# A streamed decode step on one core: the first keys in two loads, the score product ahead of the value product, and the last loads of the stream rearranged

## The chip, the core and the metric

The kernel runs on one core of a Trainium2 chip. The metric is the device time of one execution in microseconds (us). The kernel before takes 384.94 us, the median of 3 runs (384.27 to 385.3).

The core has a matrix engine (PE in the profile, with its weight loads as PEld), a vector engine (DVE), a scalar engine (ACT), a general engine (POOL) and a synchronisation engine (SP) that here only starts DMA transfers. Each engine works through its own list of instructions in order; they meet at semaphores. Data come from the chip's main memory by 16 DMA engines into the on-chip memory (SBUF); products of PE land in a small accumulator memory (PSUM).

## The reference

Two tokens (B = 2 batch rows of one position each, D = 448) are layer-normalised. The first branch is a grouped attention over a cache: 16 query heads, 8 key/value heads, 4096 cached positions, head size 256. The second is a bilinear gate. The output is `x + s * silu(h @ w_down)`:

```python
def _A_ref(x, k_cache, v_cache, wq, wo):
    ...
    scores = jnp.einsum("bhqd,bhkd->bhqk", q, k) * (Dh ** -0.5)
    p = _softmax(scores, axis=-1)
    o = jnp.einsum("bhqk,bhkd->bhqd", p, v)
    return ... @ wo
def _B_ref(x, w_gate, w_up, w_down):
    g = jnp.einsum("bsd,df->bsf", x, w_gate)
    u = jnp.einsum("bsd,df->bsf", x, w_up)
    return jnp.einsum("bsf,fd->bsd", g * u, w_down)
xn = _layernorm(x)
s = _A_ref(xn, A_k_cache, A_v_cache, A_wq, A_wo)
g = _silu(_B_ref(xn, B_w_gate, B_w_up, B_w_down))
return x + s * g
```

Everything is float32. The caches hold 2 x 8 x 4096 x 256 keys and as many values, 134 MB together; the weights are 24 MB more. Each number read takes part in one or two multiplications only.

## The kernel before, in words

**Steps.** The attention is cut into N = 16 steps, one for each pair of a key/value head and a batch row. Step i needs the keys k_i (128 x 8192 floats, 4 MB) and the values v_i (4 MB). For each step the program does:

- `scores(i)` on PE (line 344): 16 products of 128x512 from the scaled query copies `qs` (made by POOL, line 153) and k_i, into the PSUM tile `s`.
- the largest score: DVE's `maximum(i)` reduces `s` to `m` (line 242); PE turns that column to a row (`sm`, line 348); DVE reduces the row (`mx`, line 244); PE spreads it back (line 350); DVE scales and negates it (line 248).
- ACT's `exps(i)` (line 173) writes the exponentials `p` and their sums `su`; DVE adds the sums into `sr` (line 252).
- `turn(i)` on PE (line 300) transposes `p` into the two PSUM tiles `pt`, and sums the denominators (line 356). DVE copies one half to `pT` (line 255), ACT the other (line 178); DVE takes the reciprocal (line 257).
- `values(i, v)` on PE (line 366): 16 products of 128x512 from `pT` and v_i, into the PSUM tile `o`. ACT copies `o` to `ob` (line 185); `join(i)` on PE (line 374) folds it into `oc`; DVE's `heads(i)` writes the finished heads to `oT` (line 263).

**Buffers and loads.** There are two large buffers, `buf[0]` and `buf[1]`, of 8 MB each, and `low` (6.3 MB). SP issues all large loads, in one order (lines 120 to 135): the gate and up weights to `low`, `w_down` to `buf[1]`, `wq` to `buf[0]`; then the first 8 MB of the cache, which hold k_0 and k_1, to `buf[1]`; then 14 loads of 8 MB, number i holding v_i and k_(i+2), to `buf[i % 2]`; then v_14 into the first half of `buf[0]` and v_15 into the first half of `buf[1]`; then `w_o` in six pieces of 14, 9, 4, 3, 1 and 1 of its 32 steps. The first three pieces (27 steps) go to `low`, the last three to the second half of `buf[0]` (`late`).

Below, load i is the one that holds v_i and k_(i+2). SP waits ahead of a load until the buffer is free: load 0 for the query product that read `wq`, load i from 1 on for `scores(i)`, the last reader of its buffer. v_14 waits for `scores(14)`, v_15 for `scores(15)`. The `w_o` loads have no wait of their own, but stand behind these on SP.

**PE's order.** PE runs `scores(0)`, `turn(0)`, `scores(1)`, and then a hardware loop of seven passes over two steps each, whose body is for each of the two:

```python
values(i, buf[i][:, :ROW])
turn(i + 1)
join(i)
scores(i + 2, buf[i][:, ROW:])
```

`scores` includes the two small products for the largest score and their waits. After the loop come `values(14)`, `turn(15)`, `join(14)`, `values(15)` and `join(15)`.

**The end.** `w_o` is multiplied by the finished heads. Steps 0 to 26 are summed in `o` on four column groups of PE (line 305). ACT copies that sum to `ys` (line 191), and `spread` (line 309) adds it into `acc`; then the last five steps are multiplied straight into `acc` (line 419), DVE multiplies by the gate and adds x (lines 278 and 281), and SP stores the result (line 135). The order on PE is fixed by the code: 27 steps, `spread`, five steps.

## Time and profile before

| what | value |
|---|---|
| median of 3 runs | 384.94 us (384.27 to 385.3) |
| the profiled execution's own time | 384.97 us |
| its span in the profile | 383.7 us |
| read from main memory | 158.54 MB, 413 GB/s over the span |
| busy share of PE, DVE, ACT, POOL | 58%, 16%, 13%, 1% |
| mean clock granted to PE | 0.795 of full speed |

The span is the stretch from the first to the last recorded instruction; the device time of the same execution is 1.27 us longer. All times in rows of the profile count from the span's start. The waits name the engine (or DMA) whose event came last. In groups of PE's rows, each float32 product is recorded as two matmuls, so 16 products are x32. "PEq" and "issue" as releasers mean that the profile shows no event for the wait, which is where PE waits for a load's semaphore. A table of windows gives for each stretch the busy time of each engine, the clock granted to PE, the mean busy share of the 16 DMA engines and their GB/s; in it a packet counts in the window in which it starts, so windows shorter than a packet can show more than 1.00 or nothing.

### The profile page before, as it was taken

The page shows a single profiled execution, that of the slowest core. Times are in us where ns is not written, and L with a number is a line of the kernel's source. Part 1 is how long each engine was busy: PE and PEld are TensorE (multiplying, and loading weights), DVE is VectorE, ACT ScalarE, POOL GpSimd, SP SyncE. Part 2 cuts the span into 40 slices and gives each one's busy share as a digit, 9 for nine tenths or more (in the row PEclk, how much of TensorE's full clock was granted, in tenths as well). Part 3 has the DMA queues.
Part 4 walks back from the last instruction along what each step waited for, and adds up shares of the span by engine and source line. Part 5 has one row for each costly group of instructions (what it writes and reads, how often), then busy time and mean ns, then how long its engine had stood idle before and what let it go on. Part 6 is the DMA issues. An engine that isn't in the chain of part 4 may idle for free. (4 is left out here: it accounts for less than half of the span.)

```text
span 383.7 us, 3749 instructions
## 1 busy us (share of the span) xinstructions
PE 224.3 (58%) x1642; PEld 88.4 (23%) x1642; DVE 60.3 (16%) x142; ACT 48.8 (13%) x105; POOL 5.0 (1%) x23
## 2 busy tenths in 40 slices
PE   0094363579092929392939383838483847477666
PEld 0021010323040404040403141313131313132322
DVE  3001000321112121212121212120212120212100
ACT  1002020111111111111111111111111111111100
POOL 1000000000000000000000000000000000000000
PEclk9999595889686777887776877786877786878898
DMA  8999999989999999999999999999999999985993
GB/s 336 424 443 456 435 437 437 437 323 432 437 437 432 437 431 437 437 430 418 437 430 410 430 424 430 437 437 437 437 430 437 437 437 437 417 366 222 433 416 142
DMA packets 3915, 158.70 MB, mean 414 GB/s; under 512 B 578, under 2 KB 836, under 8 KB 1092
## 3 DMA queue, kind: packets, MB, share of 16 engines
q1 hardware_dynamic: 3888, 158.59, 96.4%
q8 instruction: 5, 0.08, 0.1%
q10 hardware_dynamic: 20, 0.01, 0.0%
q14 instruction: 2, 0.02, 0.0%
HBM read 158.54 MB, written 0.06 MB: 413 GB/s over the span
## 5 line engine op out<-in xcount | busy, mean ns | idle before, releaser
L366 PE MATMUL o<-buf,pT 128*32 128x512 f32 x512 | 87.0, 841 | 73.5 <-PEq L50 73.5
L344 PE MATMUL s<-buf,qs 128*32 128x512 f32 x512 | 60.7, 616 | 9.4 <-PEq L50 9.4
L366 PEld LDWEIGHTS o<-buf,pT 128*32 128x32 f32 x512 | 22.4, 149 | 125.0 <-issue 124.9
L173 ACT ACTIVATE p<-s,m 128x512 f32<-128x512 f32 x32 | 21.7, 682 | 124.9 <-DVE m L248 124.9
L255 DVE COPY pT<-pt 128x512 f32<-128x512 f32 x16 | 11.1, 692 | 133.1 <-PE pt L300 133.1
L242 DVE TENSOR_REDUCE m<-s 128x1 f32<-128x1024 f32 x16 | 19.6, 1225 | 65.8 <-PE s L344 65.8
L185 ACT COPY ob<-o 128x512 f32<-128x512 f32 x16 | 9.4, 586 | 136.8 <-PE o L366 136.8
L344 PEld LDWEIGHTS s<-buf,qs 128*32 128x32 f32 x512 | 15.5, 113 | 40.5 <-issue 40.3
L300 PE MATMUL pt<-ident,p 128*128 128x128 f32 x128 | 18.3, 289 | 2.1 <-PEq L50 2.1
L300 PEld LDWEIGHTS pt<-ident,p 128*128 128x128 f32 x128 | 14.4, 146 | 14.8 <-issue 14.8
L348 PE MATMUL sm<-ident,m 128*1 128x128 f32 x16 | 4.3, 269 | 23.0 <-PEq L50 23.0
L374 PE MATMUL oc<-sel,ob 128*128 128x2 f32 x128 | 16.5, 251 | 0.8 <-PEq L50 0.8
L374 PEld LDWEIGHTS oc<-sel,ob 128*128 128x128 f32 x128 | 15.6, 192 | 1.7 <-issue 1.7
L350 PE MATMUL sm<-one,mx 1*128 1x1 f32 x32 | 6.6, 273 | 13.8 <-PEq L50 13.8
L291 PE MATMUL s<-low,xnT 128*32 128x448 f32 x48 | 7.0, 730 | 12.5 <-DMA low<-wgu 12.5
L291 PE MATMUL s<-buf,xnT 128*32 128x512 f32 x48 | 6.9, 721 | 9.8 <-DMA buf<-wq 9.8
L244 DVE TENSOR_REDUCE mx<-sm 1x128 f32<-1x512 f32 x16 | 10.9, 678 | 7.2 <-PE sm L348 7.2
L178 ACT COPY pT<-pt 128x512 f32<-128x512 f32 x16 | 9.4, 585 | 8.6 <-PE pt L300 8.6
L348 PEld LDWEIGHTS sm<-ident,m 128*1 128x1 f32 x16 | 1.3, 79 | 37.1 <-issue 37.1
L305 PE MATMUL o<-low,oT 128*32 128x448 f32 x54 | 8.1, 684 | 2.9 <-DMA low<-wo 2.9
L350 PEld LDWEIGHTS sm<-one,mx 1*128 1x128 f32 x32 | 5.7, 222 | 16.8 <-issue 16.8
L252 DVE TENSOR_TENSOR sr<-su 128x128 f32<-128x128 f32 x16 | 4.7, 292 | 24.2 <-ACT p L173 24.2
(65 smaller groups left out, 65.8 us busy)
## 6 DMA issues: line engine op xcount, KB each, us to landing
buf<-vv SPq DMA_DIRECT2D x2, 4096.0 KB, 14.8
buf<-wq SPq DMA_DIRECT2D x1, 7168.0 KB, 42.5
low<-wgu SPq DMA_DIRECT2D x1, 6272.0 KB, 18.1
buf<-wd SPq DMA_DIRECT2D x1, 3136.0 KB, 25.1
low<-wo SPq DMA_DIRECT2D x1, 3136.0 KB, 19.7
low<-wo SPq DMA_DIRECT2D x1, 2016.0 KB, 25.1
low<-wo SPq DMA_DIRECT2D x1, 896.0 KB, 26.8
buf<-wo SPq DMA_DIRECT2D x1, 672.0 KB, 27.7
```

The lines of the kernel that those rows point to most:

```text
L173: ins = e.activation(p[:, h], s[:, h], AF.Exp, bias=m[:, 1:2], scale=1.0 / 16, accum_out=su[:, h:h + 1])
L178: e.copy(pT[:, 1], pt[1]).then_inc(sems["pt"], 1)
L185: e.copy(ob, o).then_inc(sems["ob"], 1)
L242: e.tensor_reduce(m[:, 0:1], s.rearrange("p h n -> p (h n)"), axis=AX.X, op=OP.max).then_inc(sems["m"], 1)
L244: e.tensor_reduce(mx, sm[:1, None, :128].rearrange("p o (c j) -> p o j c", c=NT).to_broadcast([1, NT, W, NT]), axis=AX.X, op=OP.max).then_ ...
L255: e.tensor_copy(pT[:, 0], pt[0]).then_inc(sems["pt"], 1)
L291: e.matmul(t[W * c:W * (c + 1), :n], xnT[:, k, :], block(NT * k + c), start=k == 0, stop=False)
L300: ins = e.transpose(t[:, i, :], a[:, i * 128:(i + 1) * 128], ident)
L344: ins = e.matmul(s[W * c:W * (c + 1), h], qs[i % 2][:, d].rearrange("p j q -> p (j q)"), k[:, h, d, c, :], start=d == 0, stop=d == 1)
L350: pe.ev(e.matmul(sm[:, 128:129], mx.rearrange("p c j -> p (c j)"), one, start=True, stop=True), "x", i)
L366: ins = e.matmul(o[W * at:W * (at + 1), :], pT[:, h, j, 64 * c + 16:64 * c + 48], v[:, h, j, c, :], start=h == 0 and j < 2, stop=h == 1 an ...
L374: ins = e.matmul(oc[:, 2 * d:2 * d + 2], ob[:, h * 256 + d * 128:h * 256 + (d + 1) * 128], sel[:, h], start=h == 0, stop=h == 1)
```

## The change

Five edits go together.

1. **The first 8 MB are two loads of 4 MB**, k_0 and k_1, each with a semaphore of its own. `scores(0)` waits for the first alone, `scores(1)` for the second.
2. **In a step of the loop, `turn(i + 1)` and `scores(i + 2)` stand ahead of `values(i)`**. The two small products for the largest score are parted from `scores` (`highest`, `spread_highest`) and stand inside the value product, after its sixth and its twelfth product. DVE and ACT follow: DVE has its reciprocal and `maximum(i + 2)` ahead of the copy to `pT`, and the sums last; ACT has `exps(i + 2)` ahead of the copy to `ob`. The copies to `pT` now come after `values(i)`, which reads `pT`.
3. **The buffers are given free by `values`**: load i waits from i = 2 on for `values(i - 2)`, since `scores(i)` has read the other half of that buffer earlier.
4. **v_14 and v_15 both go to `buf[0]`**, each with its own semaphore, once `values(12)` is done. The first three `w_o` loads follow without a wait. The last three go to the second half of `buf[1]` in place of `buf[0]` and wait for `values(13)`.
5. **At the end the three `w_o` steps of the fourth piece stand ahead of `spread`**, and only the last two steps behind it.

**PE, one step of the loop** (`o<-buf,pT` is the value product, `s<-buf,qs` the score product, `pt<-ident,p` the transposes, `oc<-sel,ob` the join; t0 is the semaphore of the load). Before:

```order
L366 MATMUL o<-buf,pT 32x512 [waits t0,pt]
L366 MATMUL o<-buf,pT 32x512 x15
L300 MATMUL pt<-ident,p 128x128 [waits sr]
L300 MATMUL pt<-ident,p 128x128 x7
L356 MATMUL sm<-sel,sr 128x2
L374 MATMUL oc<-sel,ob 128x2 [waits ob]
L374 MATMUL oc<-sel,ob 128x2 x3
L344 MATMUL s<-buf,qs 32x512 [waits q]
L344 MATMUL s<-buf,qs 32x512 x15
L348 MATMUL sm<-ident,m 1x128 [waits m]
L350 MATMUL sm<-one,mx 128x1 [waits mx]
```

With the change, the same step:

```order
L315 MATMUL pt<-ident,p 128x128 [waits pt,sr]
L315 MATMUL pt<-ident,p 128x128 x7
L375 MATMUL sm<-sel,sr 128x2
L359 MATMUL s<-buf,qs 32x512 [waits t0,q]
L359 MATMUL s<-buf,qs 32x512 x15
L384 MATMUL o<-buf,pT 32x512 x6
L365 MATMUL sm<-ident,m 1x128 [waits m]
L384 MATMUL o<-buf,pT 32x512 x6
L369 MATMUL sm<-one,mx 128x1 [waits mx]
L384 MATMUL o<-buf,pT 32x512 x4
L392 MATMUL oc<-sel,ob 128x2 [waits ob]
L392 MATMUL oc<-sel,ob 128x2 x3
```

The wait for the load has moved from the value product to the score product, the transposes of the next step stand ahead of it, and the two waits for DVE's maximum now lie within the value product.

**SP, from the cache loads to the store** (`pe` is PE's own count of finished work). Before:

```order
L124 DMA buf<-kv 128x16384 [waits pe]
L127 DMA buf<-kv 128x16384 [waits pe] x14
L130 DMA buf<-vv 128x8192 [waits pe] x2
L133 DMA low<-wo 128x6272
L133 DMA low<-wo 128x4032
L133 DMA low<-wo 128x1792
L133 DMA buf<-wo 128x1344
L133 DMA buf<-wo 128x448 x2
L135 DMA res<-r 128x112 [waits dv]
```

With the change:

```order
L125 DMA buf<-kv 128x8192 [waits pe]
L125 DMA buf<-kv 128x8192
L128 DMA buf<-kv 128x16384 [waits pe] x14
L131 DMA buf<-vv 128x8192 [waits pe]
L131 DMA buf<-vv 128x8192
L136 DMA low<-wo 128x6272
L136 DMA low<-wo 128x4032
L136 DMA low<-wo 128x1792
L136 DMA buf<-wo 128x1344 [waits pe]
L136 DMA buf<-wo 128x448 x2
L138 DMA res<-r 128x112 [waits dv]
```

The second of the last two value loads has lost its wait, and the wait ahead of the `w_o` loads now stands ahead of the fourth of them only.

**PE, the end** (`o<-low,oT` are the first 27 steps of `w_o`, `acc<-ys,pick` is `spread`, `acc<-buf,oT` the last five steps, four products each). As a piece of the difference:

```order
-L305 MATMUL o<-low,oT 32x448 x27
-L309 MATMUL acc<-ys,pick 32x112 x4
-L419 MATMUL acc<-buf,oT 32x112 x20
+L320 MATMUL o<-low,oT 32x448 x27
+L444 MATMUL acc<-buf,oT 32x112 x12
+L324 MATMUL acc<-ys,pick 32x112 x4
+L444 MATMUL acc<-buf,oT 32x112 x8
```

Twelve of the twenty products have moved ahead of `spread`.

The diff:

```diff
--- before.py
+++ after.py
@@ -59,7 +59,7 @@
 
     first = nc.alloc_semaphore("first")
     sems = {n: nc.alloc_semaphore(n) for n in (
-        "x", "xg", "gu", "wd", "wq", "t0", "t1", "pt", "sr", "ob", "q", "m", "mx", "res")}
+        "x", "xg", "gu", "wd", "wq", "k0", "k1", "v14", "v15", "t0", "t1", "pt", "sr", "ob", "q", "m", "mx", "res")}
     won = [nc.alloc_semaphore(f"wo{i}") for i in range(len(ABREAST + DIRECT))]
     pe = Queue(nc, nc.tensor, "pe", known)
     dv = Queue(nc, nc.vector, "dv", known)
@@ -103,7 +103,7 @@
     oc = ps("oc", [128, 512])
     acc = ps("acc", [128, 512])
 
-    late = buf[0][:, ROW:]
+    late = buf[1][:, ROW:]
     bounds = [0]
     for n in ABREAST + DIRECT:
         bounds.append(bounds[-1] + n)
@@ -121,14 +121,17 @@
         e.dma_start(buf[1][:, :14 * D], wd).then_inc(sems["wd"], 16)
         e.dma_start(buf[0][:, :28 * 512], wq).then_inc(sems["wq"], 16)
         sp.after(pe, "y4")
-        e.dma_start(buf[1], kv[0]).then_inc(turns[1], 16)
+        for h in range(2):
+            e.dma_start(buf[1][:, h * ROW:(h + 1) * ROW], kv[0][:, h * ROW:(h + 1) * ROW]).then_inc(sems[f"k{h}"], 16)
         for i in range(N - 2):
-            sp.after(pe, *(("q", 1) if i == 0 else ("s", i)))
+            sp.after(pe, *(("q", 1) if i == 0 else ("s", 1) if i == 1 else ("v", i - 2)))
             e.dma_start(buf[i % 2], kv[1 + i]).then_inc(turns[i % 2], 16)
-        for i in range(N - 2, N):
-            sp.after(pe, "s", i)
-            e.dma_start(buf[i % 2][:, :ROW], vv[i % 2]).then_inc(turns[i % 2], 16)
+        sp.after(pe, "v", N - 4)
+        for h in range(2):
+            e.dma_start(buf[0][:, h * ROW:(h + 1) * ROW], vv[h]).then_inc(sems[f"v{N - 2 + h}"], 16)
         for n, lo, hi in zip(won, bounds, bounds[1:]):
+            if lo == early:
+                sp.after(pe, "v", N - 3)
             t = low[:, lo * D:hi * D] if hi <= early else late[:, (lo - early) * D:(hi - early) * D]
             e.dma_start(t, wo[:, lo * D:hi * D]).then_inc(n, 16)
         sp.after(dv, "res")
@@ -181,12 +184,12 @@
         half(0)
         exps(1)
         for i in range(N):
+            if i + 2 < N:
+                exps(i + 2)
             ac.after(pe, "v", i)
             e.copy(ob, o).then_inc(sems["ob"], 1)
             if i + 1 < N:
                 half(i + 1)
-            if i + 2 < N:
-                exps(i + 2)
         ac.after(pe, "w4")
         ac.ev(e.copy(ys, o[:, :D]), "accs")
 
@@ -247,14 +250,18 @@
             dv.after(pe, "x", i)
             dv.ev(e.tensor_scalar(m[:, 1:2], sm[:, 128:129], -1.0 / 16, None, op0=OP.mult), "neg", i)
 
-        def half(i):
+        def sums(i):
             dv.after(ac, "exp", i)
             e.tensor_tensor(sr, su[:, 0:1].to_broadcast([128, 128]), su[:, 1:2].to_broadcast([128, 128]),
                             op=OP.add).then_inc(sems["sr"], 1)
+
+        def inverse(i):
+            dv.after(pe, "u", i)
+            dv.ev(e.reciprocal(r[i % 2], sm[:, 130:132]), "r", i)
+
+        def half(i):
             dv.after(pe, "t", i, 0)
             e.tensor_copy(pT[:, 0], pt[0]).then_inc(sems["pt"], 1)
-            dv.after(pe, "u", i)
-            dv.ev(e.reciprocal(r[i % 2], sm[:, 130:132]), "r", i)
 
         def heads(i):
             g, b = where(i)
@@ -266,14 +273,22 @@
                 r[i % 2][:, :, None, None].to_broadcast([128, REP, 2, DUP]), op=OP.mult), "oT", i)
 
         maximum(0)
+        sums(0)
         half(0)
+        inverse(0)
         maximum(1)
+        sums(1)
         for i in range(N):
             if i + 1 < N:
+                inverse(i + 1)
+            if i + 2 < N:
+                maximum(i + 2)
+            if i + 1 < N:
+                dv.after(pe, "v", i)
                 half(i + 1)
             heads(i)
             if i + 2 < N:
-                maximum(i + 2)
+                sums(i + 2)
         dv.after(pe, "fin")
         dv.ev(e.tensor_mul(r0, acc[:, :SL], gate), "r0")
         dv.after(dv, "r0")
@@ -304,10 +319,10 @@
             c = i % NT
             return e.matmul(t[W * c:W * (c + 1), :D], lhs, rhs, start=i < NT, stop=i >= total - NT)
 
-        def spread(stop):
+        def spread(start, stop):
             for c in range(NT):
                 ins = e.matmul(acc[W * c:W * (c + 1), :SL], pick.rearrange("p b j -> p (b j)"),
-                               ys[:, c * SL:(c + 1) * SL], start=True, stop=stop)
+                               ys[:, c * SL:(c + 1) * SL], start=start, stop=stop)
             return ins
 
         pe.after(dv, "xn")
@@ -327,7 +342,7 @@
             ins = abreast(o, hT[:, i], buf[1][:, i * D:(i + 1) * D], i, 14)
         pe.ev(ins, "y4")
         pe.after(ac, "ys")
-        pe.ev(spread(True), "y")
+        pe.ev(spread(True, True), "y")
         e.wait_ge(sems["wq"], 16)
         for h in range(2):
             pe.ev(rows(s[:, h], buf[0][:, h * 14 * 512:(h + 1) * 14 * 512], 512), "q", h)
@@ -344,8 +359,12 @@
                         ins = e.matmul(s[W * c:W * (c + 1), h], qs[i % 2][:, d].rearrange("p j q -> p (j q)"),
                                        k[:, h, d, c, :], start=d == 0, stop=d == 1)
             pe.ev(ins, "s", i)
+
+        def highest(i):
             pe.take(sems["m"])
             pe.ev(e.transpose(sm[:1, :128], m[:, 0:1], ident), "m", i)
+
+        def spread_highest(i):
             pe.take(sems["mx"])
             pe.ev(e.matmul(sm[:, 128:129], mx.rearrange("p c j -> p (c j)"), one, start=True, stop=True), "x", i)
 
@@ -355,12 +374,11 @@
                 pe.ev(turned(pt[h], p[:, h]), "t", i, h)
             pe.ev(e.matmul(sm[:, 130:132], sr, sel[:, 0], start=True, stop=True), "u", i)
 
-        def values(i, v):
-            pe.take(turns[i % 2], 16)
-            pe.take(sems["pt"], 2)
+        def values(i, v, between):
             v = v.rearrange("p (h i c n) -> p h i c n", h=2, i=BLK, c=2)
             for h in range(2):
                 for j in range(BLK):
+                    between.get((h, j), lambda: None)()
                     for c in range(2):
                         at = 2 * (j % 2) + c
                         ins = e.matmul(o[W * at:W * (at + 1), :], pT[:, h, j, 64 * c + 16:64 * c + 48],
@@ -375,18 +393,23 @@
                                    start=h == 0, stop=h == 1)
             pe.ev(ins, "j", i)
 
-        pe.take(turns[1], 16)
-        scores(0, buf[1][:, :ROW])
-        turn(0)
-        scores(1, buf[1][:, ROW:])
+        for i in range(2):
+            e.wait_ge(sems[f"k{i}"], 16)
+            scores(i, buf[1][:, i * ROW:(i + 1) * ROW])
+            highest(i)
+            spread_highest(i)
+            if i == 0:
+                turn(0)
 
         at, count = dict(pe.at), pe.n
         with nc.Fori(0, LOOPS, 1, engines=[PE], head_slot={PE: 0}):
             for i in range(2):
-                values(i, buf[i][:, :ROW])
+                pe.take(sems["pt"], 2)
                 turn(i + 1)
+                pe.take(turns[i], 16)
+                scores(i + 2, buf[i][:, ROW:])
+                values(i, buf[i][:, :ROW], {(0, 3): lambda: highest(i + 2), (1, 2): lambda: spread_highest(i + 2)})
                 join(i)
-                scores(i + 2, buf[i][:, ROW:])
         per = pe.n - count
         for key, n in list(pe.at.items()):
             if at.get(key) != n:
@@ -394,13 +417,15 @@
                     pe.at[(key[0], key[1] + 2 * k, *key[2:])] = n + per * k
         pe.n = count + per * LOOPS
 
-        i = N - 2
-        values(i, buf[0][:, :ROW])
-        turn(i + 1)
-        join(i)
-        values(i + 1, buf[1][:, :ROW])
-        pe.after(dv, "oT", i)
-        join(i + 1)
+        for i in range(N - 2, N):
+            pe.take(sems["pt"], 2)
+            if i == N - 2:
+                turn(N - 1)
+            else:
+                pe.after(dv, "oT", N - 2)
+            e.wait_ge(sems[f"v{i}"], 16)
+            values(i, buf[0][:, (i - N + 2) * ROW:(i - N + 3) * ROW], {})
+            join(i)
         pe.after(dv, "gate")
 
         def left(i):
@@ -417,11 +442,12 @@
                 else:
                     for c in range(NT):
                         ins = e.matmul(acc[W * c:W * (c + 1), :SL], left(i), wo_step(i)[:, c * SL:(c + 1) * SL],
-                                       start=False, stop=i == WO - 1)
+                                       start=lo == early and i == lo, stop=i == WO - 1)
             if hi == early:
                 pe.ev(ins, "w4")
+            if lo == early:
                 pe.after(ac, "accs")
-                spread(False)
+                spread(False, False)
         pe.ev(ins, "fin")
 
     pool_side()
```

## The prediction

> **What bounds the kernel now.** I read the DMA part of the page first, because the kernel reads 158.54 MB and PE is busy for little more than half of the span.
>
> ```profile
> DMA  8999999989999999999999999999999999985993
> GB/s 336 424 443 456 435 437 437 437 323 432 437 437 432 437 431 437 437 430 418 437 430 410 430 424 430 437 437 437 437 430 437 437 437 437 417 366 222 433 416 142
> q1 hardware_dynamic: 3888, 158.59, 96.4%
> ```
>
> Each slice is 383.7 / 40 = 9.59 us. Most stand near 437 GB/s; four stand out: the ninth (323), those from 335.7 us on (366, 222) and the last (142). The bytes are the same after the change, so time can only come from such holes, or go into new ones. Next I read PE in order of time, at the places where it starts on freshly landed data:
>
> ```profile
> 63.78 5.44 PE L344 MATMUL s<-buf,qs 128*32 128x512 f32 x32 [9.39 <-PEq L50]
> 74.29 1.94 PE L300 MATMUL pt<-ident,p 128*128 128x128 f32 x8 [2.15 <-PEq L50]
> 76.37 4.28 PE L344 MATMUL s<-buf,qs 128*32 128x512 f32 x32
> 105.64 5.00 PE L366 MATMUL o<-buf,pT 128*32 128x512 f32 x32 [7.69 <-PEq L50]
> ...
> 318.47 6.10 PE L366 MATMUL o<-buf,pT 128*32 128x512 f32 x32 [5.29 <-PEq L50]
> 326.54 3.64 PE L344 MATMUL s<-buf,qs 128*32 128x512 f32 x32
> 337.83 4.96 PE L366 MATMUL o<-buf,pT 128*32 128x512 f32 x32 [4.73 <-PEq L50]
> ...
> 361.38 5.13 PE L366 MATMUL o<-buf,pT 128*32 128x512 f32 x32 [2.90 <-PEq L50]
> 368.57 3.20 PE L305 MATMUL o<-low,oT 128*32 128x448 f32 x28 [0.24 <-DMA low<-wo]
> 374.44 4.89 PE L305 MATMUL o<-low,oT 128*32 128x448 f32 x26 [2.68 <-DMA low<-wo]
> ```
>
> The first keys are there at 63.78. `values(1)`, which waits for load 1, starts at 105.64, and `values(13)`, which waits for load 13, at 337.83: twelve loads in 232.19 us, **19.35 us for a load of 8.39 MB**, or 433 GB/s. Through the loop PE waits for DMA at every step. What is not stream lies at two places on SP:
>
> ```profile
> 80.72 0.33 SPq L127 DMA_DIRECT2D buf<-kv  x1
> ...
> 330.24 0.33 SPq L130 DMA_DIRECT2D buf<-vv  x1
> 348.45 0.33 SPq L130 DMA_DIRECT2D buf<-vv  x1
> 348.82 1.63 SPq L133 DMA_DIRECT2D low<-wo  x3
> ```
>
> and in the windows around them, where a packet counts at its start:
>
> ```profile
> 80.00:80.50 0.50, 0.50 (x8) 0.00 (x0) 0.00 (x0) 0.00 (x0) 0.00 (x0) 1.00 0.01 0
> 80.50:81.00 0.50, 0.15 (x4) 0.00 (x0) 0.27 (x1) 0.00 (x0) 0.24 (x1) 1.00 0.01 0
> 81.00:81.50 0.50, 0.00 (x0) 0.00 (x0) 0.50 (x1) 0.00 (x0) 0.00 (x0) 1.00 0.00 0
> 81.50:82.00 0.50, 0.00 (x0) 0.00 (x0) 0.46 (x1) 0.00 (x0) 0.00 (x0) 1.00 4.09 1311
> 346.00:349.00 3.00, 2.39 (x24) 0.52 (x16) 0.54 (x1) 0.00 (x0) 0.00 (x0) 1.00 0.00 0
> 349.00:349.50 0.50, 0.00 (x0) 0.00 (x0) 0.50 (x1) 0.00 (x0) 0.00 (x0) 1.00 1.20 328
> ```
>
> Load 1 is issued at 80.72, and no new packet starts from 80.0 to 81.5: some engines have run out. v_15 is issued at 348.45, and nothing starts from 346 to 349. A first packet follows its issue after about a microsecond in both. The rest is the tail, in the chain of waits:
>
> ```profile
> 374.40 0.04 issue
> 374.44 4.90 PE o L305 x26
> 379.35 0.02 issue
> 379.37 0.54 ACT ys L191
> 379.91 0.04 issue
> 379.95 0.40 PE acc L309 x8
> 380.35 1.00 PE acc L419 x40
> 381.36 0.02 issue
> ```
>
> The second `w_o` piece lands at 374.40. From the end of PE's work at 381.36 to the span's end are 2.34 us (gate, residual, store).
>
> **The change, part by part.**
>
> *First keys in two loads (gain 3.16 us).* Two loads after the keys, load 1 should land at 63.78 + 2 x 19.35 = 102.48; it landed at 105.64. The lost 3.16 us come from its late issue, which waits for `scores(1)`. With the change:
>
> ```profile
> 44.19 4.15 PE L291 MATMUL s<-buf,xnT 128*32 128x512 f32 x24 [9.80 <-DMA buf<-wq]
> 54.89 0.41 POOL L153 COPY qs<-qT 128x64 f32<-128x64 f32 x2 [49.74 <-DVE qT L237]
> ```
>
> `wq` has landed at 44.19 and k_0 follows, half a load later, at 53.9; the queries are ready at 55.3, so the query now decides. `scores(0)` takes 3.64 to 5.44 and ends at 58.9 to 60.7. Before, 5.07 us passed from its end (69.22) to `turn(0)` (74.29) and 2.08 from there to `scores(1)`, which took 4.28. That puts `scores(1)` at 66.0 to 67.9, after k_1's landing near 63.8, and the issue of load 1 at 70.3 to 72.1: 8 us before the engines ran dry, against 0.7 after. The bounds are 0 (the hole stays) and 3.16; I take all of it, since later loads, issued well ahead, run without a hole. What hides PE's part is load 0's stream up to 83.1.
>
> *The split itself (0).* One more issue on SP, 0.33 us by the rows above, while `wq` streams. Its price per load is bounded by two cases: v_15, issued into empty queues, took 361.38 - 348.45 = 12.93 us where half of 19.35 is 9.67, so 3.26 more. Loads that stand in the queue behind each other are these:
>
> ```profile
> low<-wgu SPq DMA_DIRECT2D x1, 6272.0 KB, 18.1
> buf<-wd SPq DMA_DIRECT2D x1, 3136.0 KB, 25.1
> ```
>
> They were issued 0.42 us apart and landed 7.4 us apart, which is 3.21 MB at 433 GB/s: no price. The two key loads are issued back to back, so 0; 3.26 is the other end. The Trainium skill, "DMA: Bandwidth & Descriptors", section "Anatomy of one DMA — SWDGE (gpsimd) path", fits about 2.0 us fixed plus bytes at 436 GB/s per transfer, on another path than SP's; were that paid, the split would cost 2.0 us and the sum be 379.0, but it makes an 8.39 MB load 21.2 us where the trace has 19.35.
>
> *The step's new order (0).* A load now waits for `values(i - 2)`, which starts only after `scores(i)` and holds two waits for DVE. The longest rows give 5.44 + 6.10, and the whole chain of the largest score, were none of it covered, adds 74.29 - 69.22 = 5.07 at most: 16.6 us after a landing at worst, 3.64 + 4.96 = 8.6 at best. Before, it was 330.24 - 318.47 = 11.8. The next issue has until 19.35 - 1.1 = 18.2. So the stream covers it in every case, and if not, each microsecond beyond costs one at each step. Queued behind PE's waits are only the value product and, after it, the join and the next transposes, which with their waits took 1.97 us before (324.57 to 326.54), and now also a copy to `pT` ahead of the transposes:
>
> ```profile
> L255 DVE COPY pT<-pt 128x512 f32<-128x512 f32 x16 | 11.1, 692 | 133.1 <-PE pt L300 133.1
> ```
>
> These 2.7 us end at 11.3 to 19.3 us after the landing, ahead of the next one.
>
> *The last values and `w_o` (gain 4.20 us).* v_14 and v_15 hold 8.39 MB, one load's worth; they landed 361.38 - 337.83 = 23.55 us after load 13, 4.20 more than 19.35. Now both are issued after `values(12)`, some 10 us after load 12, so behind load 13 in the queue, and three `w_o` pieces with them; v_14's empty stretch has no place to appear. Bounds 0 and 4.20; smaller rows don't cut it, since v_14 before (32 KB rows) had started its last packet 8.2 us after load 13. The last three pieces wait for `values(13)`, at most 16.6 us after load 13 lands at 334.7, so by 351; ahead of them v_15 and the first pieces stream until about 369.
>
> *The tail (gain 0.60 us).* All that follows v_15's landing keeps its order: its product, the join, 14 steps on the first piece, a gap, 13 steps on the next two pieces. Twelve of 20 products (0.60 of the 1.00 us) move from behind ACT's copy to beside it. The upper bound depends on PE's clock:
>
> ```profile
> 371.77:374.44 2.67, 0.00 (x0) 0.00 (x0) 0.00 (x0) 0.00 (x0) 0.00 (x0) 1.00 0.92 381
> 374.44:379.35 4.91, 4.89 (x26) 1.35 (x26) 0.00 (x0) 0.00 (x0) 0.00 (x0) 0.65 0.59 237
> ```
>
> After 2.67 us of idleness PE ran the 13 steps at a mean clock of 0.65, in 4.91 us; the 14 before them took 3.20. At full clock 13 take 2.97, 1.94 less. But the last `w_o` piece then decides: the pieces of one step took 27.8 us from issue,
>
> ```profile
> 350.50 1.53 SPq L133 DMA_DIRECT2D buf<-wo  x3
> buf<-wo SPq DMA_DIRECT2D x2, 224.0 KB, 27.8
> ```
>
> so the last landed near 379.4, 18.0 after v_15. With v_15 at 354.0 it lands at 372.0; eight products (0.40) and 2.34 make 374.8, against 375.7 with the slow clock. I take the slow clock, since the gap between the first two pieces stays as it was.
>
> Sum: 383.7 - 3.16 - 4.20 - 0.60 = 375.7 us of span. The profiled execution took 384.97, 1.27 beyond its span, and lies within 0.03 of the median, so **377.0 us**.
>
> **The rivals.** (a) *PE keeps its clock in the tail*: the last load decides, 374.8 + 1.27 = 376.1. For it: the gap is short. Against it: in this trace it was enough. The Trainium skill, "TensorE: Matmul & The Clock Gate", section "Part 1: The HAM clock gate", has the clock fall after an idle window of about 3.4 us, counted in windows that run freely; 2.67 us would often pass, and the trace shows one that did not. (b) *The first hole stays*, because the two halves pay the 3.26 us of a fresh start or load 1 is issued late anyway: about 380.2. Against it: the 8 us of lead. (c) *The last hole stays*, because SP cannot queue six loads ahead: 377.0 + 4.2 = 381.2. Against it: seven loads were issued within 3.6 us from 348.45. (d) *Slower: PE's step becomes the bound.* If the wait for the largest score inside the value product, with DVE's copies behind it, makes a landing-to-release time of over 18.2 us, every later load is late. Loads 2 to 13 wait so, twelve of them: at 18.9 us the 8.0 us of gain are gone (0.66 each), and at 19.0 the time is about 386.6, where I have 8.6 to 16.6. (e) *The stream fills the old holes with slower packets* and nothing moves: 385. Nothing in the rows speaks for it.
>
> **How the numbers follow.** Forecast 0.53, (a) 0.30, (b) 0.07, (c) 0.05, (d) 0.03, (e) 0.02. The range is 374.8 to 379.2: below (a) by the 1.1 us by which `w_o`'s 7.34 MB at 433 GB/s (16.9 us) would be quicker than the 18.0 above, and 0.2 for runs that differ; above by a first term of which only a third is saved. (b) to (e) lie outside, 0.17. Measurements of this kernel tell some 0.3% from no change, 1.2 us: faster 0.95, same 0.02 (e), slower 0.03 (d).
>
> **What would show it.** Load 1 issued near 71; its first use (now a score product) near 102.5, and then one every 19.35 to 334.7; v_15's product near 354.0; no window of 2 us without packets before 370; the 13 steps near 367 with a clock below 0.7, or else above 0.9 and PE waiting for the last piece. Steps longer than 19.5 us, or a load issued more than 18 us after a landing, would make it wrong.

## The result, and the profile after

The changed kernel takes **375.95 us** (median of 4 runs, 375.19 to 376.1) against 384.61 us for the kernel before (median of 4, 383.91 to 385.3). The ratio is 0.977, with a 95% interval of 0.975 to 0.980: 8.7 us less. The prediction was 377.0, with 374.8 to 379.2 as its range; rival (a), PE keeping its clock in the tail, had 376.1. The profiled execution took 375.19 us and has a span of 373.9, 9.8 less than the span before.

The page's DMA lines of the changed kernel, in slices of 373.9 / 40 = 9.35 us:

```profile
DMA  8999999999999999999999999999999999999995
GB/s 339 421 461 425 428 414 445 443 436 449 435 443 407 428 436 428 442 442 443 435 407 442 428 435 435 449 449 407 428 435 428 449 435 449 421 393 442 426 413 213
q1 hardware_dynamic: 4032, 158.59, 98.5%
```

The two holes of before (323 in the ninth slice; 366 and 222 near the end) are gone; between the first slice and the last none is under 393. The bytes are the same. PE in order of time, where it starts on new data (L359 is the score product, L384 the value product, L320 the first 27 steps of `w_o`, L444 the last five):

```profile
55.75 3.64 PE L359 MATMUL s<-buf,qs 128*32 128x512 f32 x32 [0.87 <-PEq L50]
66.74 4.47 PE L359 MATMUL s<-buf,qs 128*32 128x512 f32 x32
83.19 6.47 PE L359 MATMUL s<-buf,qs 128*32 128x512 f32 x32 [4.75 <-PEq L50]
102.54 5.34 PE L359 MATMUL s<-buf,qs 128*32 128x512 f32 x32 [3.71 <-PEq L50]
...
334.75 5.29 PE L359 MATMUL s<-buf,qs 128*32 128x512 f32 x32 [3.76 <-PEq L50]
...
349.81 4.58 PE L384 MATMUL o<-buf,pT 128*32 128x512 f32 x32
356.55 3.64 PE L384 MATMUL o<-buf,pT 128*32 128x512 f32 x32 [0.32 <-DVE oT L270]
361.94 3.20 PE L320 MATMUL o<-low,oT 128*32 128x448 f32 x28
366.21 3.19 PE L320 MATMUL o<-low,oT 128*32 128x448 f32 x26 [1.07 <-DMA low<-wo]
370.08 0.78 PE L444 MATMUL acc<-buf,oT 128*32 128x112 f32 x24 [0.67 <-DMA buf<-wo]
```

Load 0 is used at 83.19, load 1 at 102.54 (forecast 102.5), load 13 at 334.75 (forecast 334.7): again (334.75 - 102.54) / 12 = 19.35 us for a load. Two things differ from the forecast. `values(15)` starts at 356.55, released by DVE and not by its data, so PE is late there and not the load. And the 13 steps at 366.21 take 3.19 us, after a gap of 1.07 us, where they took 4.89 behind a gap of 2.67. SP's issues:

```profile
71.28 0.33 SPq L128 DMA_DIRECT2D buf<-kv  x1
...
326.93 0.80 SPq L131 DMA_DIRECT2D buf<-vv  x2
327.78 1.38 SPq L136 DMA_DIRECT2D low<-wo  x3
345.15 1.28 SPq L136 DMA_DIRECT2D buf<-wo  x3
```

Load 1 is issued at 71.28 (80.72 before), v_15 at about 327.3 (348.45 before). The chain of waits now ends in the last loads:

```profile
345.15 24.88 DMA buf<-wo
370.03 0.04 issue
370.08 0.78 PE acc L444 x24
370.86 0.19 PE acc L324 x8
371.05 0.54 PE acc L444 x16
371.59 0.02 issue
```

Before, it ran through the second `w_o` piece, 4.90 us of PE and ACT's copy. Three stretches can be read in the traces, and the table compares them: the time at which load 1 is used; from the use of load 13 to the landing of the second `w_o` piece (the 23rd step); and from there to the span's end.

| trace | load 1 used | load 13 used | to the 23rd step | from there to the end | span |
|---|---|---|---|---|---|
| before | 105.64 | 337.83 | 36.57 | 9.3 | 383.7 |
| changed | 102.54 | 334.75 | 31.42 | 7.7 | 373.9 |
| difference | 3.10 | 3.08 | 5.15 | 1.6 | 9.8 |

### The profile page after: what moved, and what is told of

It is laid out like the page before. It is cut to its first block, busy times and chain, and to the rows that moved or that the text cites. A ratio compares the mean times of both kernels' runs of the same rounds, so it can differ in the third digit from the quotient of the medians.

```text
span 373.9 us, 3748 instructions
## 1 busy us (share of the span) xinstructions
PE 245.5 (66%) x1642; PEld 95.2 (25%) x1642; DVE 60.4 (16%) x142; ACT 45.7 (12%) x105; POOL 5.0 (1%) x23
## 5 line engine op out<-in xcount | busy, mean ns | idle before, releaser
L359 PE MATMUL s<-buf,qs 128*32 128x512 f32 x512 | 90.4, 870 | 57.9 <-PEq L50 57.9
L384 PE MATMUL o<-buf,pT 128*32 128x512 f32 x512 | 76.5, 606 | 0.3 <-DVE oT L270 0.3
L359 PEld LDWEIGHTS s<-buf,qs 128*32 128x32 f32 x512 | 22.7, 152 | 111.4 <-issue 111.4
L315 PE MATMUL pt<-ident,p 128*128 128x128 f32 x128 | 21.6, 325 | 12.8 <-PEq L50 12.8
L384 PEld LDWEIGHTS o<-buf,pT 128*32 128x32 f32 x512 | 17.0, 110 | 33.0 <-issue 30.6
L315 PEld LDWEIGHTS pt<-ident,p 128*128 128x128 f32 x128 | 17.1, 164 | 13.7 <-issue 13.7
L156 POOL COPY qs<-qT 128x64 f32<-128x64 f32 x16 | 3.7, 236 | 293.5 <-PE s L359 243.1
L320 PE MATMUL o<-low,oT 128*32 128x448 f32 x54 | 6.4, 544 | 1.1 <-DMA low<-wo 1.1
L375 PEld LDWEIGHTS sm<-sel,sr 128*128 128x128 f32 x32 | 7.0, 270 | 0.0
L176 ACT ACTIVATION_READ_ACCUMULATOR p<-s,m 128x1 f32 x32 | 6.3, 196 | 0.0
```

The source lines that it names most:

```text
L176: ins = e.activation(p[:, h], s[:, h], AF.Exp, bias=m[:, 1:2], scale=1.0 / 16, accum_out=su[:, h:h + 1])
L315: ins = e.transpose(t[:, i, :], a[:, i * 128:(i + 1) * 128], ident)
L359: ins = e.matmul(s[W * c:W * (c + 1), h], qs[i % 2][:, d].rearrange("p j q -> p (j q)"), k[:, h, d, c, :], start=d == 0, stop=d == 1)
L384: ins = e.matmul(o[W * at:W * (at + 1), :], pT[:, h, j, 64 * c + 16:64 * c + 48], v[:, h, j, c, :], start=h == 0 and j < 2, stop=h == 1 an ...
```

## The experiments

Each median stands beside runs of the kernel before on the same chip. Their median was 384.48 us (27 runs) for the four kernels made from before, 384.33 us (9 runs) for the changed kernel with the old order, with the old place of `spread`, with its gap filled and with the pieces cut 7, 16, 4 (first runs), and 384.33 us (11 runs) for the remaining ones.

**The first keys in two loads, alone.**

```diff
-e.dma_start(buf[1], kv[0]).then_inc(turns[1], 16)
+for h in range(2):
+    e.dma_start(buf[1][:, h * ROW:(h + 1) * ROW], kv[0][:, h * ROW:(h + 1) * ROW]).then_inc(sems[f"k{h}"], 16)
 ...
-pe.take(turns[1], 16)
+e.wait_ge(sems["k0"], 16)
 scores(0, buf[1][:, :ROW])
 turn(0)
+e.wait_ge(sems["k1"], 16)
 scores(1, buf[1][:, ROW:])
```

> The kernel before with the first edit alone: k_0 and k_1 are two loads with a semaphore each. Theory (the first hole is the late issue of load 1): load 1 is issued near 71 us and values(1) starts near 102.5 instead of 105.64; everything behind it, with its own holes, is 3.1 us earlier: 381.5 us against 384.6. Rival (the hole lies elsewhere, or is given back by the price of one more load): values(1) still near 105.6 and 384.6 us, or later by up to 3.3.

382.38 us (12 runs); ratio 0.994, 0.992 to 0.996. PE and SP in its trace:

```profile
72.58 0.33 SPq L128 DMA_DIRECT2D buf<-kv  x1
...
346.68 0.33 SPq L131
```

```profile
102.55 6.29 PE L367 MATMUL o<-buf,pT 128*32 128x512 f32 x32 [5.09 <-PEq L50]
...
334.79 6.22 PE L367 MATMUL o<-buf,pT 128*32 128x512 f32 x32 [5.17 <-PEq L50]
...
366.76 3.20 PE L306 MATMUL o<-low,oT 128*32 128x448 f32 x28
372.70 3.19 PE L306 MATMUL o<-low,oT 128*32 128x448 f32 x26 [2.73 <-DMA low<-wo]
```

Load 1 is there at 102.55, as forecast, and load 13 at 334.79, so the first hole is closed by this edit alone, and the extra load cost nothing that can be seen. Line 131 issues v_15. The median fell by 2.1, not 3.1, and the trace (381.53 us, span 380.2) shows what else moves. Against the first trace of before, load 13 is 3.04 us earlier; 1.30 us are given back at the second hole, where 37.87 us pass from load 13 to the second `w_o` piece (372.66), because `values(13)` took 6.22 us against 4.96 and v_15 was issued 11.89 us after load 13 instead of 10.62; and the tail is 1.8 us shorter. There the 13 steps ran in 3.19 us behind a gap of 2.73 us, longer than the one behind which they took 4.89. So the length of the gap alone does not decide whether the clock in the tail falls.

**The last loads, alone.**

```diff
-late = buf[0][:, ROW:]
+late = buf[1][:, ROW:]
 ...
-for i in range(N - 2, N):
-    sp.after(pe, "s", i)
-    e.dma_start(buf[i % 2][:, :ROW], vv[i % 2]).then_inc(turns[i % 2], 16)
+sp.after(pe, "s", N - 2)
+for h in range(2):
+    e.dma_start(buf[0][:, h * ROW:(h + 1) * ROW], vv[h]).then_inc(sems[f"v{N - 2 + h}"], 16)
 for n, lo, hi in zip(won, bounds, bounds[1:]):
+    if lo == early:
+        sp.after(pe, "s", N - 1)
 ...
```

(PE's last two value products wait for the new semaphores, and the last one reads `buf[0]`.)

> The kernel before with the fourth edit alone: v_14 and v_15 both to buf[0] after scores(14), the first three w_o pieces behind them, the last three to buf[1] after scores(15); the old step order stays. Theory (the hole at 346 to 349 us is the wait of v_15 and nothing of the step order is needed to close it): no empty stretch there, v_15 there near 357.2, 4.2 us earlier. PE's own chain (small products to 351.5, values(14), transposes, join) then reaches values(15) near 358.5, after its data, so the idle gap between the first two w_o pieces shrinks from 2.7 to about 1.8 us: if the clock holds 378.4 us, if it falls 380.3. Rival (the step order is what lets the loads go early): 383 us or more.

378.31 us (6 runs); ratio 0.984, 0.982 to 0.987. PE in its trace:

```profile
336.82 5.81 PE L371 MATMUL o<-buf,pT 128*32 128x512 f32 x32 [5.47 <-PEq L50]
...
358.49 3.64 PE L371 MATMUL o<-buf,pT 128*32 128x512 f32 x32
...
363.88 3.20 PE L307 MATMUL o<-low,oT 128*32 128x448 f32 x28
368.28 3.19 PE L307 MATMUL o<-low,oT 128*32 128x448 f32 x26 [1.20 <-DMA low<-wo]
```

The second piece lands (368.24) 31.42 us after load 13, just as in the changed kernel. `values(15)` starts at 358.49, on the microsecond that PE's own chain gave, and the gap shrinks to 1.20. The theory holds with the clock kept, the old step order suffices, and the edit is worth 6.2 us, more than the 4.2 of the prediction's term; in the trace the stretch is 5.15 us shorter than in the first one of before, and the tail (375.9 - 368.24 = 7.7) 1.6.

**The step's order, alone** (second and third edits; the loop as in the diff of the change, the rest as before, except that the waits are these):

```diff
-for i in range(N - 2, N):
-    sp.after(pe, "s", i)
+for i in range(N - 2, N):
+    sp.after(pe, "v", i - 2)
```

> The kernel before with the second and third edits alone: scores ahead of the value product, loads wait for values(i - 2); the first keys are one load, v_14 and v_15 go to two buffers after values(12) and values(13), the last w_o pieces to buf[0], spread ahead of all five last steps. Theory (the stream hides the step's order in every step): 384.6 us within 0.7, a step every 19.35 us, both holes still there, since load 1 still waits for scores(1) and v_15 now for values(13), which ends about 10.4 us after load 13. Rival (the order itself brings part of the gain): 382.5 us or less.

383.42 us (12 runs); ratio 0.997, 0.995 to 0.999. Both holes are in its trace: load 1 is used at 104.86, and the second piece comes 37.56 us after load 13. The gap before it is 1.97 us and the 13 steps take 3.19. The gain of 1.1 us lies between what the two sides expected. Against the first trace of before, load 1 is used 0.8 us earlier, the stretch to the second piece is 1.0 longer and the tail (7.6) 1.7 shorter; the steps are no shorter. The shorter tail would make the gain if it comes up in more runs than with the old order; one trace cannot show that, so the cause of the 1.1 us stays open.

**Filling PE's gap in the kernel before.**

```diff
 ins = abreast(o, left(i), wo_step(i), i, early)
+if i == ABREAST[0] - 1:
+    for k in range(FILL):   # FILL = 10
+        abreast(s[:, 0], left(k % 4), wo_step(k % 4), k, FILL)
```

> The kernel before with ten more products on PE between the first and the second w_o piece; they repeat operands that are there and write a tile that nobody reads any more. Nothing of the result changes. Theory (the tail's 13 steps are slow because PE's clock falls in the 2.67 us gap): no gap, clock 1.0, the 13 steps take 3.0 us instead of 4.9, then the last piece near 379.3 decides; 383.4 us, 1.2 less. Rival (the clock does not follow the gap): 384.6 or up to 0.3 more.

382.75 us (10 runs); ratio 0.995, 0.993 to 0.997. In its trace the 13 steps take 3.19 us, and from the second piece to the end 7.7:

```profile
372.51 2.76 PE L306 MATMUL s<-low,oT 128*32 128x448 f32 x18
375.84 3.19 PE L306 MATMUL o<-low,oT 128*32 128x448 f32 x26 [0.56 <-DMA low<-wo]
```

More work on PE made the kernel faster by 1.7 us in the median. Eight of the ten runs stand at a mean clock of 0.798 or 0.799 and took 382.22 to 383.3 us; the other two, at 0.790 and 0.791, took 384.22 and 384.96. None of the 27 runs of before beside them is above 0.795. That is what a clock that falls with PE's idleness would give, and the 1.6 us by which 9.3 differs from 7.7 would be the price of the slow tail. The trace itself doesn't show it: it is of the slowest of the ten runs, 384.96 us, as long as before in spite of its fast tail, because load 13 was used only at 338.01 and the second piece came 37.78 us later. And the 13 steps took 3.19 us without any filling too, in the traces of the three experiments above and in the next one.

**A second trace of the kernel before**, unchanged.

> The kernel before, unchanged, for a second trace of its end. Theory (the phase of PE's clock, not the program, sets how long v_15's wait and the 13 steps on the second and third w_o piece take): the 2.7 us gap between the pieces is there again, and behind it the 13 steps take either 3.2 us at clock 1.0 or 4.9 us at about 0.65; from load 13's landing to the second piece 36.5 to 37.9 us, more where values(13) ran slower. Rival (the first trace's values belong to the program): 4.9 us and 36.6 us again, within 0.1.

The execution took 382.67 us, with a span of 381.4:

```profile
104.26 5.97 PE L366 MATMUL o<-buf,pT 128*32 128x512 f32 x32 [6.15 <-PEq L50]
336.47 5.92 PE L366 MATMUL o<-buf,pT 128*32 128x512 f32 x32 [5.47 <-PEq L50]
...
368.03 3.20 PE L305 MATMUL o<-low,oT 128*32 128x448 f32 x28
373.68 3.19 PE L305 MATMUL o<-low,oT 128*32 128x448 f32 x26 [2.44 <-DMA low<-wo]
```

The same program, with a gap of 2.44 us, now kept its clock and did the 13 steps in 3.19 us. The first hole was smaller (104.26 with the first keys used at 63.51: 40.75 us, against 41.86 in the first trace), the second was larger (37.16 against 36.57), with `values(13)` at 5.92 us against 4.96 and v_15 issued 11.58 us after load 13. So the sizes of all three terms belong to one execution; the theory stands, the rival falls.

**The changed kernel with the old step order and the old release** (the second and third edits undone, the others kept).

```diff
-pe.take(sems["pt"], 2)
-turn(i + 1)
-pe.take(turns[i], 16)
-scores(i + 2, buf[i][:, ROW:])
-values(i, buf[i][:, :ROW], {(0, 3): lambda: highest(i + 2), (1, 2): lambda: spread_highest(i + 2)})
+values(i, buf[i][:, :ROW])
+turn(i + 1)
 join(i)
+scores(i + 2, buf[i][:, ROW:])
 ...
```

(SP waits for `scores(i)` again, the last loads for `scores(14)` and `scores(15)`; DVE and ACT have their old order.)

> The changed kernel with the old step order (value product, transposes, join, then scores) and the old release by scores(i); the two key loads, the placing of the last loads and the new place of spread stay. Theory (order and release are worth nothing, the stream covers them): 376.0 us within 0.6; load 1 issued near 71, its data used near 102.5, v_15 near 354.0. Rival (the order keeps PE's end short): 377.5 us or more.

375.24 us (5 runs); ratio 0.976, 0.974 to 0.979, not to be told from the changed kernel's 0.977, and 0.2 us below the range that was expected. Load 1 is used at 102.60 and load 13 at 334.83; the chain of waits ends in the same last loads:

```profile
361.47 8.01 PE L308 MATMUL o<-low,oT 128*32 128x448 f32 x54 [0.68 <-DMA low<-wo]
370.11 0.78 PE L426 MATMUL acc<-buf,oT 128*32 128x112 f32 x24 [0.63 <-DMA buf<-wo]
```

In this trace the 27 steps took 8.01 us, with PE's clock at 0.50 until after 364 us, and still PE stood idle for 0.63 us until the last loads: they decide the end, and not PE. The order of the step is worth nothing that these runs can tell here, once the two holes are closed.

**The changed kernel with `spread` ahead of all five last steps.**

```diff
-if lo == early:
-    pe.after(ac, "accs")
-    spread(False, False)
+    pe.after(ac, "accs")   # now under: if hi == early
+    spread(False)
```

> The changed kernel with spread again ahead of all five last steps. Theory (the last w_o piece, near 371.0 us, decides the end, and ACT's copy is done at 370.0): 376.0 us within 0.4. The prediction's term (the twelve products lie on the chain): 0.6 us more, 376.6.

375.62 us (5 runs); ratio 0.977, 0.974 to 0.979: nothing lost. From the second piece (365.97) to the end are 7.7 us here too. The 0.6 us of the prediction are not there.

**Filling the 1.07 us gap of the changed kernel** (the same lines as above, FILL = 4).

> The changed kernel with four more products on PE in the 1.07 us gap between the first two w_o pieces, on operands that are there, into a tile that nobody reads. Theory (the clock already holds over this gap and the last load decides): 376.0 us within 0.4. Rival (in part of the runs the clock falls even here, which is why they spread from 375.2 to 376.1): all runs near 375.2.

375.83 us (5 runs, 375.51 to 376.05). Nothing was gained, and the runs did not draw together near 375.2, as the rival would have it. In the trace the 13 steps ran at full speed:

```profile
366.84 3.19 PE L321 MATMUL o<-low,oT 128*32 128x448 f32 x26 [1.13 <-DMA low<-wo]
```

A wait of 1.13 us is left in spite of the four products, because the second piece landed 32.31 us after load 13 (334.49 to 366.80) instead of 31.42. That made this execution longer than the profiled one of the changed kernel; where the 0.9 us come from is not known.

**A longer gap in the changed kernel**, by cutting the pieces 7, 16, 4; then a second trace of the same; then the same with the gap filled (FILL = 8).

```diff
-ABREAST = (14, 9, 4)
+ABREAST = (7, 16, 4)
```

> The changed kernel with the w_o pieces cut 7, 16, 4 in place of 14, 9, 4: the same bytes in the same order, but PE has only 7 steps (1.6 us) to do while the second piece lands, so it is idle for about 2.6 us, and 20 steps follow. Theory (a gap of that length lets the clock fall, whatever made it): clock below 0.7 behind the gap, the 20 steps take 6.5 us, PE decides the end: 377.7 to 378.3 us. Rival (the clock holds): 20 steps in 4.6 us, 376.6 us at most.

> The changed kernel with the w_o pieces cut 7, 16, 4, as before, for a second trace, since its runs fell into two groups, near 375.3 us at a mean clock of 0.799 and 376.8 to 377.6 at 0.791. Theory (PE's clock falls behind the gap in some runs): a run near 377 shows the steps behind the gap at a clock below 0.75 in 5.5 to 6.5 us; one near 375.3 shows them in 4.0 to 4.6 us. Rival (the groups come from the loads): the second piece lands more than a microsecond later in a slow run.

> The changed kernel with the w_o pieces cut 7, 16, 4 and eight more products on PE in the gap (1.8 us, repeated operands, into a tile that nobody reads). Theory (the clock alone makes the slow group of the cut without them): one group, all runs 375.2 to 376.2 us. Rival (the group comes from something else, such as later loads): two groups as before, some runs above 376.7.

The kernel with the pieces cut 7, 16, 4 has a median of 376.79 us (ratio 0.980, 0.977 to 0.983). Its five runs took 375.2 and 375.39 us at a mean granted clock of 0.799, and 376.79, 377.4 and 377.64 at 0.791. Both traces are of short executions (375.2 and, the second, 375.48, at 0.795). The first:

```profile
334.67 6.47 PE L359 MATMUL s<-buf,qs 128*32 128x512 f32 x32 [4.20 <-PEq L50]
...
363.10 1.70 PE L320 MATMUL o<-low,oT 128*32 128x448 f32 x14
366.14 3.96 PE L320 MATMUL o<-low,oT 128*32 128x448 f32 x40 [1.33 <-DMA low<-wo]
```

PE came 1.2 us later to the first piece than in the trace of the changed kernel (363.10 against 361.94), so the gap was 1.33 us (1.65 in the second trace) and not the 2.6 that I had expected. PE's speed in the steps before sets it: the score product on load 13 took 6.47 us here and 5.29 there. With the gap filled, the six runs took 375.7 to 376.73 us, none at 0.791. That fits a clock that falls in some runs. But the two longest of the six, 376.25 and 376.73 us, lie above the range of the theory at a clock of 0.800, and the longest is one that the rival named. No trace shows one of the three long runs of the unfilled kernel, so what made them long stays open.

**The first and the third weight load in two each.**

```diff
-e.dma_start(low, wgu).then_inc(sems["gu"], 16)
+for h in range(2):
+    e.dma_start(low[:, h * 14 * FC:(h + 1) * 14 * FC], wgu[:, h * 14 * FC:(h + 1) * 14 * FC]).then_inc(sems["gu"], 16)
```

(and `wq` likewise; PE waits for 32.)

> The changed kernel with the first and the third weight load cut into two each (rows of 25 and 28 KB in place of 50 and 57). The holes are closed, so what is left of the stream below 433 GB/s is its first 44.2 us: 16.97 MB, 39.2 us at that rate. Theory (long rows of these sizes are carried more slowly: 50 KB packets start every 1.95 us, against 1.85 at 433 GB/s): wq is there about 1.5 us earlier and the time is 374.5 us. Rival (it is the start itself, the second packets that follow only 2.3 us after the first): wq near 44.1 again and 376.0 us.

375.49 us (6 runs); ratio 0.977, 0.974 to 0.979. `wq` is used at 44.02, against 44.17 in the changed kernel. The length of the rows is not what the first 44 us lose, and in this the rival holds; the time is 0.5 us under its 376.0, within what the kernels here differ by that keep the changed kernel's loads (375.24 to 375.95).

## Why the prediction was right, and where its sizes were off

**First keys, 3.16 us:** right in place and cause. Load 1 was issued at 71.28 (forecast 70.3 to 72.1) and used at 102.54 (forecast 102.48), and with this edit alone at 102.55. The size belongs to the trace that I read: in the second trace of before the hole was 40.75 - 38.70 = 2.05 us, and alone the edit gave 2.1 us in the median. The lateness of the issue does not give the size by itself: load 1 was issued 16.94 us after the first keys were used in the first trace of before (hole 3.16) and 17.37 us after in the second (hole 2.05).

**The split, 0 us:** right. Load 0 is used at 83.19, where 63.78 + 19.35 gives 83.13. The 3.26 us of a fresh start were not paid; both loads stood in a full queue. The 2.0 us per transfer that the Trainium skill, "DMA: Bandwidth & Descriptors", section "Anatomy of one DMA — SWDGE (gpsimd) path", fits for another path do not show here either.

**The step's order, 0 us:** right in the changed kernel. The steps are 19.35 us apart as before, `values(13)`, which gives its buffer free, ends 10.4 us after load 13's landing (334.75 to 345.14; forecast 8.6 to 16.6), and undoing the order changes nothing that can be measured. Alone, in the kernel before, the order gave 1.1 us that this term doesn't have and that no run explains.

**The last values and `w_o`, 4.20 us:** the mechanism is right, the term was too small, and so was its upper bound. I sized the hole at v_15's landing (361.38). Read at the second `w_o` piece, which the chain of waits named, it is 5.15 us in the same trace, and 5.7 to 6.5 in other traces of kernels that still have it. The stream that restarts at 349 us goes on being late behind v_15; which packets make that last microsecond was not taken apart. Closed, the stretch is 31.42 us, and nothing is left in it: 8.39 MB of values and 23 of the 32 `w_o` steps (5.28 MB) take 31.6 us at 433 GB/s.

**The tail, 0.60 us:** wrong in its reason. I took the slow clock "since the gap between the first two pieces stays as it was", and the twelve products as saved time. The gap did not stay: with v_15 in time PE itself became late (`values(15)` at 356.55, behind `join(14)` and DVE, where load 13's 334.75 and 19.35 for the next 8.39 MB make 354.1), so that the first piece was multiplied later against the stream, 4.23 us ahead of the second piece's landing in place of 5.83, and the gap shrank to 1.07 us. PE kept its clock, and the last piece decides the end, as in rival (a). It landed at 370.03, 2.0 us ahead of that rival's 372.0: the 18.0 us that `w_o` took behind v_15 in the first trace held about a microsecond of the same hole, the 5.15 less 4.20; the rest of the 2.0 is not explained. There the twelve products lie beside a wait, so their new place gave nothing (0.977 without it). The gain in the tail was 1.6 us against the first trace of before, and 0.1 against its second (7.8).

The sum 3.08 + 5.15 + 1.6 is the 9.8 us of the two profiled spans; the medians differ by 8.7, because the profiled execution of the changed kernel was the quickest of its four, 0.76 us under their median, and before's was 0.36 above its own. That the forecast came so near is luck in part: alone, the first keys gave 2.1 us in place of 3.16 and the last loads 6.2 in place of 4.20, errors of opposite sign, and the 0.60 of the tail stood on a slow clock that did not come. For **rivals (b), (c), (d) and (e)** nothing was found: no hole stayed, no step of the loop was longer than 19.4 us, and no slice between the first and the last fell under 393 GB/s.

## What to carry to other kernels

When a kernel is bound by its stream of loads, list the places where SP waits for work that hangs on the load just landed, and give each buffer its successor earlier, or put the last transfers where they wait for older work; two such places held some 8 us here (2.1 and 6.2 alone), while a reordering of the compute that looked like the core of the change gave 1.1 us alone and nothing beside the other edits. Size such a hole where the path that sets the end meets the stream again, not at the first load behind it. And before trusting a term below 2 us, take a second trace of the same kernel: what PE's clock did in one execution here was not a property of the program.

## What the runs showed of the hardware that was not expected

PE's clock can fall behind an idle gap of 2.67 us and hold over one of 2.73 or 2.44 us, in the same stretch of the program: 4.89 us against 3.19 for the same 26 recorded matmuls. The windows of the first trace of before show when it fell and came back (the clock is the third number from the right):

```profile
374.25:374.50 0.25, 0.06 (x4) 0.06 (x8) 0.00 (x0) 0.00 (x0) 0.00 (x0) 1.00 1.15 473
374.75:375.00 0.25, 0.25 (x4) 0.00 (x0) 0.00 (x0) 0.00 (x0) 0.00 (x0) 0.50 0.85 351
377.75:378.00 0.25, 0.25 (x5) 0.01 (x1) 0.00 (x0) 0.00 (x0) 0.00 (x0) 0.50 0.10 36
378.25:378.50 0.25, 0.25 (x5) 0.08 (x1) 0.00 (x0) 0.00 (x0) 0.00 (x0) 1.00 0.08 29
```

It stayed at 1.00 for the first products behind the gap, stood at 0.50 from about 374.7 to 378.1, and came back in the midst of steady work. In the changed kernel the score products that start on loads 0 to 5 take 6.47, 5.34, 5.90, 6.46, 5.32 and 5.89 us, the same three lengths in turn, though the loop's body repeats after two steps; so the clock follows a rhythm other than the program's. The Trainium skill, "TensorE: Matmul & The Clock Gate", section "Part 1: The HAM clock gate", says that the windows in which idleness is measured run freely, and puts the fall after an idle window of about 3.4 us. The traces agree with the first; a fall some 2.9 us after the last product before the gap (371.77 to about 374.7) is earlier than the second.

The clock reached the loads, too. `values(13)` took 4.96, 5.92 and 6.22 us in the two traces of before and in the one with the first keys in two loads, at a mean clock of 0.73, 0.61 and 0.58, and v_15 was issued 10.62, 11.58 and 11.89 us after load 13. The 47 runs of before beside the experiments spread from 382.95 to 386.74 us; the 14 of them at a mean clock of 0.785 to 0.787 all took over 385.3, and all others less. Of the changed kernel and the three variants that keep its loads and pieces, all 19 runs lie between 375.0 and 376.1. That fits a change that took away a dependence as well as time, but no trace shows one of the 14 longest runs of before, so it is inferred.
